# Two cached-attention blocks on one core: where x is transposed for the query projection

## The chip, the core and the metric

One core of a Trainium2 chip runs the whole kernel. The core has a matrix engine (TensorE, PE in the profile, with its weight loads shown apart as PEld), a vector engine (VectorE, DVE), a scalar engine (ScalarE, ACT), a general engine (GpSimd, POOL) and a sync engine (SyncE, SP) that here only issues DMAs. Each engine runs its own list of instructions in order; they wait for one another through semaphores. All data lies in HBM at first; DMAs bring it into SBUF (128 partitions), matmuls write into PSUM (8 banks), and PSUM is read out by VectorE or ScalarE.

The metric is the time of one execution on the device, in microseconds (us): 959.31 us as the median of three runs of the kernel before (958.41 to 959.53).

## The reference

There are two independent blocks, A and B, with the same shapes and their own data; their results are put side by side in the last dimension.

```python
B, Sq, D = 16, 64, 640;  H, Sk, Dh = 32, 512, 128
q = (x @ wq).reshape(B, Sq, H, Dh).transpose(0, 2, 1, 3)
scores = jnp.einsum("bhqd,bhkd->bhqk", q, k_cache) * (Dh ** -0.5)
p = softmax(scores, axis=-1)
o = jnp.einsum("bhqk,bhkd->bhqd", p, v_cache)
out = o.transpose(0, 2, 1, 3).reshape(B, Sq, H * Dh) @ wo      # for A and for B
```

All is bf16. K and V of both blocks are 268 MB of the 295 MB that the core reads, so each element of K and V is loaded once and used once.

## The kernel before

**Tiling.** Two batch rows of 64 queries make one tile of 128 queries. A *step* is one head for such a pair; a *macro step* m is two heads. 16 heads make a *group* of eight macro steps, eight pairs of batch rows make a *pass*, and there are four passes: block A with heads 0 to 15, A with heads 16 to 31, then B in the same way. That gives 32 groups and 256 macro steps. The weights `wq` and `wo` of a pass stay in SBUF for all its groups, in two sets of buffers. The output projection adds up over the 16 heads of a group in PSUM. In the first half of the heads the partial output is kept in SBUF (OVP on ScalarE, L555); in the second half VectorE adds it to the new one (OVF, L560) and ScalarE's queue stores the result.

**A macro step.** The operations, by the names that the code uses: KX transposes K on TensorE (L433), KE evicts it on VectorE (L442). QP2 is the query projection of two heads, ten matmuls (L451), which read x in transposed form from `xT_ring`; QE2 evicts it on ScalarE (L459). SM2 forms the scores (L467); MX takes the negative row maximum on VectorE (L476), EX the exponential with its row sum on ScalarE (L482), RC2 the reciprocal on VectorE (L488), NM the normalization on GpSimd (L496). TR2 transposes the probabilities on TensorE (L505), TE2 evicts them on VectorE (L512), PV2 multiplies with V (L524), OE2 evicts on ScalarE (L532) and OP2 is the output projection (L540 and L545).

**x.** Once in a group, LDX loads the 128 x 640 tile of x as it lies in HBM into `xn_ring`, which has one buffer (NXN = 1). XT transposes it on TensorE in five 128 x 128 pieces into the PSUM bank that TR2 uses too (PTB), and XE copies them on ScalarE into one of the two buffers of `xT_ring` (NX = 2). The group's eight QP2 read them there.

**Order on the engines.** The order on each engine is a written template (PE_T, ACT_T, DVE_T and POOL_T, L30 to L33), run once for every value of a counter k. An entry such as ("QP2", 4) emits the operation for macro step k + 4. On TensorE an iteration is TR2 of k+1, QP2 of k+4, the first half of KX of k+4, SM2 of k+3, PV2 of k+1, XT where one is due, OP2 of k, and the second half of KX of k+4. XT for the group that begins at macro step 8g runs in iteration 8g - 10 (XLEAD = 10), six iterations before its first QP2, between PV2 and OP2.

**Order of the loads.** All loads are issued by SP, in an order that a small planner works out ahead (L189 to L236). Each load has a time at which its buffer should be free, and a due time, both counted in macro steps, and an assumed duration (DMA_NS, L36). The planner's clock begins four steps before the earliest due time. It always takes the load with the earliest due time among those whose buffer is free by its clock (and a small number, the third field, breaks ties), and moves the clock on by the assumed duration. So the due times of x also set where the clock begins. K and V come in chunks of four heads, two DMAs of 512 KB each; five chunks of each fit into the rings (NKB, NVB). The weights come in eight DMAs of 640 KB per pass, as early as the planner finds room.

**Waits.** Dependencies follow from the buffers that each operation reads and writes (L266 to L286). A load waits on SP for the last reader of the buffer that it overwrites: for LDX that is XT of the group before; for K it is KX, for V it is PV2. SP runs in order, so a load that waits holds up all loads behind it.

Of the kernel before, what the change touches and what calls it, by code (L numbers as in the profile page):

```python
# [5 lines left out]
BF16 = mybir.dt.bfloat16  # L6
# [8 lines left out]
class Cfg:  # L15
    G = 4
    HH = 16
    NKB = 5
    NVB = 5
    NX = 2  # L20
    NXN = 1
    XLEAD = 10
    NQ = 2
    NKT = 2
    NP = 4
# [1 line left out]
    NT = 2  # L27
    NO = 2
    NR = 8
    PE_T = (("TR2", 1), ("QP2", 4), ("KX", 4, 0), ("SM2", 3), ("PV2", 1), ("XT", 0), ("OP2", 0), ("KX", 4, 1))  # L30
    ACT_T = (("QE2", 4), ("OE2", 1), ("XE", 0), ("EX", 3, 0), ("EX", 3, 1), ("OV", 0), ("ST", -1))
    DVE_T = (("TE2", 1), ("RC2", 2), ("KE", 4, 0), ("MX", 3, 0), ("MX", 3, 1), ("KE", 4, 1), ("OVF", 0))
    POOL_T = (("NM", 0, 0), ("NM", 0, 1))  # L33
    TAIL_SPLIT = 2
# [4 lines left out]
class Op:  # L39
# [3 lines left out]
    def __init__(self, eng, kind, idx, reads=(), writes=(), dur=0.0, ts=None, aux=None):  # L43
# [13 lines left out]


STAGES = ("LDW", "LDX", "LDK", "LDV", "KX0", "KE0", "KX1", "KE1", "QP2", "QE2", "SM2", "MX0", "MX1", "EX0", "EX1",
          "RC2", "NM0", "NM1", "TR2", "TE2", "XT", "XE", "PV2", "OE2", "OP2", "OV", "ST")  # L60
STAGE_IDX = {s: i for i, s in enumerate(STAGES)}
SUB_KINDS = ("KX", "KE", "EX", "NM", "MX")

# [1 line left out]
def build_plan(dims, cfg):  # L65
# [32 lines left out]
    def make_op(kind, m, sub):  # L98
        g0, g1 = 2 * m, 2 * m + 1
        ps_, bp, grp, h0 = step_info(g0)  # L100
        c = g0 // G
        if kind == "KX":
            return mk("pe", "KX", (m, sub), [("kn", c % cfg.NKB, g0 % G), ("kn", c % cfg.NKB, g1 % G), ("ident",)],
                      [("KTB",)], "KX%d" % sub, m, sub)
        if kind == "KE":
            return mk("dve", "KE", (m, sub), [], [("KTB",), ("ktp", m % cfg.NKT, sub)], "KE%d" % sub, m, sub)
        if kind in ("MX", "EX", "NM"):
            g = 2 * m + sub
            r = g % cfg.NR
            if kind == "MX":  # L110
                return mk("dve", "MX", g, [], [("SB", sub), ("negmax", r)], "MX%d" % sub, m, sub)
            if kind == "EX":
                return mk("act", "EX", g, [("negmax", r)], [("SB", sub), ("p", g % cfg.NP), ("rowsum", r)],
                          "EX%d" % sub, m, sub)
            return mk("pool", "NM", g, [("p", g % cfg.NP), ("recip", r)], [("pn", g % cfg.NPN)], "NM%d" % sub, m, sub)
        r0, r1 = g0 % cfg.NR, g1 % cfg.NR
        if kind in ("XT", "XE"):
            mt = m + cfg.XLEAD
            if mt % MPG != 0 or not (0 <= mt < NMAC):
                return None  # L120
            gq = mt // MPG
            m_ts = mt - cfg.XLEAD + OFF["TR2"]
            if kind == "XT":
                return mk("pe", "XT", gq, [("xn", gq % cfg.NXN), ("ident",)], [("PTB",)], "XT", m_ts, aux=gq)
            return mk("act", "XE", gq, [], [("PTB",), ("xT", gq % cfg.NX)], "XE", m_ts, aux=gq)
        if kind == "QP2":
            return mk("pe", "QP2", m, [("xT", grp % cfg.NX), ("wq", ps_ % 2, h0 // G)], [("QB",)], "QP2", m)
        if kind == "QE2":
            return mk("act", "QE2", m, [], [("QB",), ("qT", m % cfg.NQ)], "QE2", m)
        if kind == "SM2":  # L130
            return mk("pe", "SM2", m, [("qT", m % cfg.NQ), ("ktp", m % cfg.NKT, 0), ("ktp", m % cfg.NKT, 1)],
                      [("SB", 0), ("SB", 1)], "SM2", m)
        if kind == "RC2":
            return mk("dve", "RC2", m, [("rowsum", r0), ("rowsum", r1)], [("recip", r0), ("recip", r1)], "RC2", m)
        if kind == "TR2":
            return mk("pe", "TR2", m, [("pn", g0 % cfg.NPN), ("pn", g1 % cfg.NPN), ("ident",)], [("PTB",)], "TR2", m)
        if kind == "TE2":
            return mk("dve", "TE2", m, [], [("PTB",), ("pT", m % cfg.NT)], "TE2", m)
        if kind == "PV2":
            return mk("pe", "PV2", m, [("pT", m % cfg.NT), ("v", c % cfg.NVB, g0 % G), ("v", c % cfg.NVB, g1 % G)],  # L140
                      [("OB",)], "PV2", m)
        if kind == "OE2":
            return mk("act", "OE2", m, [], [("OB",), ("oT", m % cfg.NO)], "OE2", m)
        if kind == "OP2":
            return mk("pe", "OP2", m, [("oT", m % cfg.NO), ("wo", ps_ % 2, h0 // G)], [("OUTB",)], "OP2", m)
        if kind in ("OV", "OVF", "ST"):
            if h0 + 1 != SPB - 1:
                return None
            last_half = ps_ % NHALF == NHALF - 1
            if kind == "OV":  # L150
                if NHALF == 1:
                    return mk("act", "OV", m, [], [("OUTB",), ("out_sb", grp % 2)], "OV", m, aux=grp)
                if last_half:
                    return None
                return mk("act", "OVP", m, [], [("OUTB",), ("outp", bp)], "OV", m, aux=grp)
            if kind == "OVF":
                if NHALF == 1 or not last_half:
                    return None
                return mk("dve", "OVF", m, [("outp", bp)], [("OUTB",), ("out_sb", grp % 2)], "OV", m, aux=grp)
            if NHALF == 1 or not last_half:  # L160
                return None
            return mk("act", "ST", m, [("out_sb", grp % 2)], [("out_dram", grp)], "ST", m, aux=grp)
        raise ValueError(kind)

    templates = {"pe": cfg.PE_T, "dve": cfg.DVE_T, "pool": cfg.POOL_T, "act": cfg.ACT_T}
    for eng, tmpl in templates.items():
        offs = [t[1] for t in tmpl] + [cfg.XLEAD]
        for k in range(-max(offs), NMAC - min(offs)):
            for t in tmpl:
                kind, off = t[0], t[1]  # L170
                sub = t[2] if len(t) > 2 else 0
                if kind in ("XT", "XE"):
                    op = make_op(kind, k, 0)
                    if op is not None:
                        progs[eng].append(op)
                    continue
                m = k + off
                if 0 <= m < NMAC:
                    op = make_op(kind, m, sub)
                    if op is not None:  # L180
                        progs[eng].append(op)
                        if op.kind == "OV":
                            progs[eng].append(mk("act", "ST", m, [("out_sb", op.aux % 2)], [("out_dram", op.aux)],
                                                 "ST", m, aux=op.aux))
# [20 lines left out]
                                                       aux=(ps_, j), dur=cfg.DMA_NS["LDWO"] * G / 8.0)))  # L205
    for grp in range(NGRP):
        m0 = MPG * grp
        op = mk("sp", "LDX", grp, [], [("xn", grp % cfg.NXN)], "LDX", m0 - cfg.XLEAD + OFF["TR2"], aux=grp,
                dur=cfg.DMA_NS["LDX"])
        ready = NEG if grp < cfg.NXN else MPG * (grp - cfg.NXN) - cfg.XLEAD  # L210
        loads.append((ready, m0 - cfg.XLEAD - 1, 1, op))

    def chunk_pieces(c):
        if c == NCHUNK - 1 and cfg.TAIL_SPLIT > 1:
# [132 lines left out]
def mha_kernel(nc, blocks, out, cfg=None):  # L347
# [15 lines left out]
    prune_waits(progs)  # L363
    NBP, SPB, NHALF = info["NBP"], info["SPB"], info["NHALF"]
    HH = SPB
    NKB, NVB, NX, NXN, NQ, NKT, NP, NPN, NT, NO, NR = (cfg.NKB, cfg.NVB, cfg.NX, cfg.NXN, cfg.NQ, cfg.NKT, cfg.NP,
                                                       cfg.NPN, cfg.NT, cfg.NO, cfg.NR)

    def step_info(g):
# [8 lines left out]
    with contextlib.ExitStack() as es:  # L378
# [6 lines left out]
        wo_sb = sb("wo_sb", [128, 2, HH, DN], BF16)  # L385
        outp = sb("outp", [128, NBP, DN], F32) if NHALF > 1 else None
        xT_ring = sb("xT_ring", [128, NX, KT, 128], BF16)
        xn_ring = sb("xn_ring", [128, NXN, D], BF16)
        kn_ring = sb("kn_ring", [128, NKB, 2, G // 2, 8, DH], BF16)
        v_ring = sb("v_ring", [128, NVB, 2, G, 4, DH], BF16)  # L390
        ktp_ring = sb("ktp_ring", [128, NKT, 2, 2, SK], BF16)
# [202 lines left out]
        def em_LDX(e, op):  # L594
            blk, bp = grp_info(op.aux)
            src = blocks[blk][0][2 * bp:2 * bp + 2].rearrange("b q d -> (b q) d")
            ins = e.dma_start(xn_ring[:, op.aux % NXN, :], src)
            return ins, ins

        def em_XT(e, op):  # L600
            gq = op.aux
            first = last = None
            for kt in range(KT):
                ins = e.transpose(pt_ps_flat[:, kt * 128:(kt + 1) * 128],  # L604
                                  xn_ring[:, gq % NXN, kt * 128:(kt + 1) * 128], ident[:, :])
                first = first or ins
                last = ins
            return first, last

        def em_XE(e, op):  # L610
            gq = op.aux
            ins = e.activation(xT_ring[:, gq % NX].rearrange("p k q -> p (k q)"), pt_ps_flat[:, 0:KT * 128],
                               ACTF.Copy)
            return ins, ins

        def em_LDKV(e, op):
# [6 lines left out]
            else:  # L623
# [4 lines left out]

        emitters = dict(KX=em_KX, KE=em_KE, QP2=em_QP2, QE2=em_QE2, SM2=em_SM2, MX=em_MX, EX=em_EX, RC2=em_RC2,
                        NM=em_NM, TR2=em_TR2, TE2=em_TE2, PV2=em_PV2, OE2=em_OE2, OP2=em_OP2, OV=em_OV,  # L630
                        OVP=em_OVP, OVF=em_OVF, ST=em_ST, XT=em_XT, XE=em_XE, INIT1=em_INIT1, INIT2=em_INIT2,
                        LDWQ=em_LDWQ, LDWO=em_LDWO, LDX=em_LDX, LDK=em_LDKV, LDV=em_LDKV)

        def run_program(e, prog, final_waits=()):
# [85 lines left out]
```

## Time and profile before

| what | value |
|---|---|
| median of 3 runs | 959.31 us (958.41 to 959.53) |
| profiled execution, first to last instruction (span) | 956.8 us |
| TensorE (PE) | 919.4 us busy, 96% |
| VectorE (DVE) | 841.9 us, 88% |
| ScalarE (ACT) | 567.1 us, 59% |
| GpSimd (POOL) | 416.9 us, 44% |
| transposes of x, 160 on TensorE | 14.4 us busy, 222 ns each |
| their evictions, 32 on ScalarE | 22.5 us busy, 702 ns each |
| loads of x, 32 on SP | 160 KB each, 2.5 / 4.3 / 10.5 us from issue to landing (least, median, most) |
| all DMAs | 299.51 MB, 313 GB/s on average |
| granted TensorE clock | 0.998 of full speed |

The profile is of one execution, taken by the hardware. Of that execution the page gives the span; what lies before its first and after its last instruction isn't shown, and the span is 2.5 us below the median of the runs. "Busy" of an engine is the time that its instructions took; "idle before" in a group's line is the time that its engine stood still just before them, with what ended it. In a line such as `ps<-ident,xn_ring` the tile written stands left of the arrow, those read to the right. SPq is the list of DMA issues on SP. A DMA's time "to landing" runs from its issue to the moment when its data is there.

### The profile page before, as it was taken

The numbers are of one execution on the slowest core, as the hardware profiler recorded it, in microseconds if no ns is written. First come the engines' busy times: TensorE is split into PE (matmuls) and PEld (weight loads), VectorE is DVE, ScalarE is ACT, GpSimd is POOL, SyncE is SP. The second block draws the span as 40 slices with busy tenths as digits, with TensorE's granted clock in tenths as the row PEclk, the third lists the DMA queues.
The fourth block names the chain that finished last, engine by engine and source line by source line (L and its number), as shares of the span: only waits on it lengthen the run. The fifth ranks groups of instructions, "written<-read, shape, count | busy, mean of one in ns | idle before, by whom it ended". The sixth has DMA issues, their size and how long they took to land.

```text
span 956.8 us, 34351 instructions
## 1 busy us (share of the span) xinstructions
PE 919.4 (96%) x14755; PEld 733.5 (77%) x15008; DVE 841.9 (88%) x1552; ACT 567.1 (59%) x1585; POOL 416.9 (44%) x518
## 2 busy tenths in 40 slices
PE   4999999999999999999999999999999999999997
PEld 3877777778777777877777787777877778777775
DVE  2898899898899999899999899889899998999996
ACT  1666656666665565656566666666666656565654
POOL 0444444444444444444444444444444444444443
PEclk9999999999999999999999999999999999999999
DMA  9999999999999999888999999988888988899830
GB/s 315 364 365 364 351 365 367 365 368 351 338 337 337 343 330 315 299 292 305 322 332 352 326 353 327 306 294 296 302 305 288 308 301 297 295 297 314 295 124 15
DMA packets 230871, 299.51 MB, mean 313 GB/s; under 512 B 9536, under 2 KB 165184, under 8 KB 230720
## 3 DMA queue, kind: packets, MB, share of 16 engines
q1 hardware_dynamic: 228416, 294.69, 91.0%
q8 instruction: 118, 1.93, 0.8%
q10 hardware_dynamic: 2304, 2.62, 0.8%
q14 instruction: 33, 0.27, 0.1%
HBM read 294.65 MB, written 2.62 MB: 311 GB/s over the span
## 4 chain that ended last, share of the span: by engine, by line
PE 89%; DVE 4%; POOL 3%; issue 2%; SPq 1%; DMA 1%; POOLq 0%; DVEq 0%
PE ps L433 22%; PE ps L524 14%; PE ps L451 14%; PE ps L467 14%; PE ps L505 12%; PE ps L545 7%; PE ps L540 5%; POOL pn_ring L496 3%; DVE out_sb L560 1%; DVE ktp_ring L442 1%; DVE pT_ring L512 1%; PE ps L604 1%; DMA xn_ring<-in_A_x_dram 1%; SPq L626 1%; SPq L583 1%
## 5 line engine op out<-in xcount | busy, mean ns | idle before, releaser
L496 POOL TENSOR_SCALAR pn_ring<-p_ring,recip 128x512 bf16<-128x512 bf16 x512 | 416.3, 843 | 532.7 <-DVE recip L488 532.7
L442 DVE COPY ktp_ring<-ps 128x1024 bf16<-128x1024 bf16 x512 | 353.7, 691 | 105.3 <-PE ps L433 85.1
L482 ACT ACTIVATE p_ring<-ps,negmax 128x512 bf16<-128x512 f32 x512 | 345.6, 684 | 4.8 <-DVE negmax L476 4.8
L476 DVE TENSOR_REDUCE negmax<-ps 128x1 f32<-128x512 f32 x512 | 327.3, 681 | 0.4 <-PE ps L467 0.3
L433 PE MATMUL ps<-ident,kn_ring 128*128 128x128 bf16 x4096 | 314.6, 220 | 2.8 <-DMA kn_ring<-in_A_k_cache_dram 1.6
L532 ACT ACTIVATE oT_ring<-ps 128x256 bf16<-128x256 f32 x256 | 98.0, 383 | 306.0 <-PE ps L524 306.0
L433 PEld LDWEIGHTS ps<-ident,kn_ring 128*128 128x128 bf16 x4096 | 251.9, 98 | 34.2 <-DVE ktp_ring L442 2.6
L524 PEld LDWEIGHTS ps<-pT_ring,v_ring 128*128 128x128 bf16 x4096 | 133.5, 98 | 109.2 <-issue 100.0
L451 PE MATMUL ps<-xT_ring,wq_sb 128*128 128x128 bf16 x2560 | 186.4, 220 | 3.2 <-DMA wq_sb<-in_A_wq_dram 3.2
L512 DVE COPY pT_ring<-ps 128x1024 bf16<-128x1024 bf16 x256 | 174.5, 682 | 4.6 <-PE ps L505 3.8
L524 PE MATMUL ps<-pT_ring,v_ring 128*128 128x64 bf16 x4096 | 163.8, 194 | 3.3 <-issue 1.7
L467 PE MATMUL ps<-ktp_ring,qT_ring 128*64 128x512 bf16 x1024 | 159.8, 392 | 0.4 <-ACT p_ring L482 0.4
L505 PE MATMUL ps<-ident,pn_ring 128*128 128x128 bf16 x2048 | 156.7, 219 | 3.5 <-POOL pn_ring L496 3.5
L451 PEld LDWEIGHTS ps<-xT_ring,wq_sb 128*128 128x128 bf16 x2560 | 155.2, 98 | 3.5 <-DMA wq_sb<-in_A_wq_dram 3.5
L459 ACT ACTIVATE qT_ring<-ps 128x256 bf16<-128x256 f32 x256 | 98.4, 384 | 66.8 <-PE ps L451 66.8
L505 PEld LDWEIGHTS ps<-ident,pn_ring 128*128 128x128 bf16 x2048 | 124.1, 98 | 7.0 <-POOL pn_ring L496 6.7
L545 PE MATMUL ps<-wo_sb,oT_ring 128*128 128x128 bf16 x512 | 112.1, 219 | 13.4
L482 ACT ACTIVATION_READ_ACCUMULATOR p_ring<-ps,negmax 128x1 f32 x512 | 105.0, 205 | 0.0
L540 PE MATMUL ps<-wo_sb,oT_ring 128*128 128x512 bf16 x259 | 97.8, 379 | 0.0
L540 PEld LDWEIGHTS ps<-wo_sb,oT_ring 128*128 128x128 bf16 x512 | 50.1, 98 | 30.6 <-ACT oT_ring L532 0.3
L467 PEld LDWEIGHTS ps<-ktp_ring,qT_ring 128*64 128x64 bf16 x1024 | 36.1, 108 | 27.1 <-ACT p_ring L482 0.6
L545 PEld LDWEIGHTS ps<-wo_sb,oT_ring 128*128 128x128 bf16 x512 | 50.1, 98 | 0.0
(13 smaller groups left out, 112.7 us busy)
## 6 DMA issues: line engine op xcount, KB each, us to landing
kn_ring<-in_A_k_cache_dram SPq DMA_DIRECT2D x128, 512.0 KB, 7.0
v_ring<-in_A_v_cache_dram SPq DMA_DIRECT2D x128, 512.0 KB, 7.2
kn_ring<-in_B_k_cache_dram SPq DMA_DIRECT2D x126, 512.0 KB, 4.8
v_ring<-in_B_v_cache_dram SPq DMA_DIRECT2D x126, 512.0 KB, 5.7
wq_sb<-in_A_wq_dram SPq DMA_DIRECT2D x8, 640.0 KB, 10.4
wo_sb<-in_A_wo_dram SPq DMA_DIRECT2D x8, 640.0 KB, 10.2
wq_sb<-in_B_wq_dram SPq DMA_DIRECT2D x8, 640.0 KB, 8.4
wo_sb<-in_B_wo_dram SPq DMA_DIRECT2D x8, 640.0 KB, 7.5
```

What stands on the lines that cost most here:

```text
L433: ins = e.transpose(kt_ps[:, t8, :], kn_ring[:, c % NKB, j, hp, t8, :], ident[:, :])
L442: ins = e.tensor_copy(dst, src)
L451: ins = e.matmul(q_ps[:, sub * 128:(sub + 1) * 128], wq_sb[:, ps_ % 2, kt, hh * DH:(hh + 1) * DH], xT_ring[:, grp % NX, kt, :], start=(kt ...
L467: ins = e.matmul(s_bank(sub)[64 * j:64 * j + 64, :], qT_ring[:, m % NQ, sub, 64 * j:64 * j + 64], ktp_ring[:, m % NKT, sub, j, :], start=T ...
L476: ins = e.reduce_max(negmax[:, r:r + 1], s_bank(g % 2), axis=AX.X, negate=True)
L482: ins = e.activation(p_ring[:, g % NP, :], s_bank(g % 2), ACTF.Exp, bias=negmax[:, r:r + 1], scale=1.0, accum_out=rowsum[:, r:r + 1])
L496: ins = e.tensor_scalar(dst, src, recip[:, r:r + 1], 1.0, ALU.mult, ALU.mult)
L505: ins = e.transpose(pt_ps[:, sub, t, :], pn_ring[:, g % NPN, t * 128:(t + 1) * 128], ident[:, :])
L512: ins = e.tensor_copy(pT_ring[:, m % NT].rearrange("p s t q -> p (s t q)"), pt_ps_flat)
L524: ins = e.matmul(o_ps[:, col:col + 64], v_ring[:, c % NVB, j, gi, t, :], pT_ring[:, m % NT, sub, t, 64 * j:64 * j + 64], start=(t == 0), s ...
L540: ins = e.matmul(out_ps0, oT_ring[:, m % NO, sub, :], wo_sb[:, ps_ % 2, hh, 0:N0], start=(hh == 0), stop=(hh == SPB - 1))
L545: last = e.matmul(out_ps1, oT_ring[:, m % NO, sub, :], wo_sb[:, ps_ % 2, hh, N0:DN], start=(hh == 0), stop=(hh == SPB - 1))
```

## The change

LDX becomes a transposing DMA: it reads the same 128 x 640 tile of x from HBM and writes it in transposed form into `xT_ring`, where QP2 reads it. `xn_ring`, XT on TensorE and XE on ScalarE go. LDX now waits for the last QP2 that read the `xT_ring` buffer which it overwrites (two groups back), where before it waited for XT. In the planner, x may be loaded ahead for two groups at the start, is due four macro steps before its group's first QP2 is emitted, and goes ahead of everything with the same due time. The first due time of all loads moves from -11 to -8 by this.

```diff
-    NXN = 1
-    XLEAD = 10
+    XLEAD = 4
...
-    PE_T = (("TR2", 1), ("QP2", 4), ("KX", 4, 0), ("SM2", 3), ("PV2", 1), ("XT", 0), ("OP2", 0), ("KX", 4, 1))
-    ACT_T = (("QE2", 4), ("OE2", 1), ("XE", 0), ("EX", 3, 0), ("EX", 3, 1), ("OV", 0), ("ST", -1))
+    PE_T = (("TR2", 1), ("QP2", 4), ("KX", 4, 0), ("SM2", 3), ("PV2", 1), ("OP2", 0), ("KX", 4, 1))
+    ACT_T = (("QE2", 4), ("OE2", 1), ("EX", 3, 0), ("EX", 3, 1), ("OV", 0), ("ST", -1))
...
     for grp in range(NGRP):
         m0 = MPG * grp
-        op = mk("sp", "LDX", grp, [], [("xn", grp % cfg.NXN)], "LDX", m0 - cfg.XLEAD + OFF["TR2"], aux=grp,
-                dur=cfg.DMA_NS["LDX"])
-        ready = NEG if grp < cfg.NXN else MPG * (grp - cfg.NXN) - cfg.XLEAD
-        loads.append((ready, m0 - cfg.XLEAD - 1, 1, op))
+        op = mk("sp", "LDX", grp, [], [("xT", grp % cfg.NX)], "LDX", m0, aux=grp, dur=cfg.DMA_NS["LDX"])
+        ready = NEG if grp < cfg.NX else MPG * (grp - cfg.NX + 1) - 1 - OFF["QP2"]
+        loads.append((ready, m0 - OFF["QP2"] - cfg.XLEAD, -1, op))
...
-        xn_ring = sb("xn_ring", [128, NXN, D], BF16)
...
             src = blocks[blk][0][2 * bp:2 * bp + 2].rearrange("b q d -> (b q) d")
-            ins = e.dma_start(xn_ring[:, op.aux % NXN, :], src)
-            return ins, ins
-
-        def em_XT(e, op):
-            gq = op.aux
-            first = last = None
-            for kt in range(KT):
-                ins = e.transpose(pt_ps_flat[:, kt * 128:(kt + 1) * 128],
-                                  xn_ring[:, gq % NXN, kt * 128:(kt + 1) * 128], ident[:, :])
-                first = first or ins
-                last = ins
-            return first, last
-
-        def em_XE(e, op):
-            gq = op.aux
-            ins = e.activation(xT_ring[:, gq % NX].rearrange("p k q -> p (k q)"), pt_ps_flat[:, 0:KT * 128],
-                               ACTF.Copy)
+            ins = e.dma_start_transpose(xT_ring[:, op.aux % NX, :, :], src)
             return ins, ins
```

More of the change, by code (lines that the diff above doesn't have):

```diff
@@ L59 @@
 STAGES = ("LDW", "LDX", "LDK", "LDV", "KX0", "KE0", "KX1", "KE1", "QP2", "QE2", "SM2", "MX0", "MX1", "EX0", "EX1",
-          "RC2", "NM0", "NM1", "TR2", "TE2", "XT", "XE", "PV2", "OE2", "OP2", "OV", "ST")
+          "RC2", "NM0", "NM1", "TR2", "TE2", "PV2", "OE2", "OP2", "OV", "ST")
 STAGE_IDX = {s: i for i, s in enumerate(STAGES)}
@@ L116, in make_op @@
         r0, r1 = g0 % cfg.NR, g1 % cfg.NR
[L117 to L125, printed above, removed]
         if kind == "QP2":
@@ L166, in build_plan @@
     for eng, tmpl in templates.items():
-        offs = [t[1] for t in tmpl] + [cfg.XLEAD]
+        offs = [t[1] for t in tmpl]
         for k in range(-max(offs), NMAC - min(offs)):
@@ L171, in build_plan @@
                 sub = t[2] if len(t) > 2 else 0
[L172 to L176, printed above, removed]
                 m = k + off
@@ L365, in mha_kernel @@
     HH = SPB
-    NKB, NVB, NX, NXN, NQ, NKT, NP, NPN, NT, NO, NR = (cfg.NKB, cfg.NVB, cfg.NX, cfg.NXN, cfg.NQ, cfg.NKT, cfg.NP,
+    NKB, NVB, NX, NQ, NKT, NP, NPN, NT, NO, NR = (cfg.NKB, cfg.NVB, cfg.NX, cfg.NQ, cfg.NKT, cfg.NP,
                                                        cfg.NPN, cfg.NT, cfg.NO, cfg.NR)
@@ L630, in mha_kernel @@
                         NM=em_NM, TR2=em_TR2, TE2=em_TE2, PV2=em_PV2, OE2=em_OE2, OP2=em_OP2, OV=em_OV,
-                        OVP=em_OVP, OVF=em_OVF, ST=em_ST, XT=em_XT, XE=em_XE, INIT1=em_INIT1, INIT2=em_INIT2,
+                        OVP=em_OVP, OVF=em_OVF, ST=em_ST, INIT1=em_INIT1, INIT2=em_INIT2,
                         LDWQ=em_LDWQ, LDWO=em_LDWO, LDX=em_LDX, LDK=em_LDKV, LDV=em_LDKV)
```

## The prediction

> **What bounds the kernel now.** First the page: engine shares and the chain of work that ended last.
>
> ```profile
> span 956.8 us, 34351 instructions
> PE 919.4 (96%) x14755; PEld 733.5 (77%) x15008; DVE 841.9 (88%) x1552; ACT 567.1 (59%) x1585; POOL 416.9 (44%) x518
> PE 89%; DVE 4%; POOL 3%; issue 2%; SPq 1%; DMA 1%; POOLq 0%; DVEq 0%
> ```
>
> TensorE is busy 96% of the span and carries 89% of the chain. What it runs in order sets the time, and work taken out of its list can be worth its length there. Next, the groups of instructions that go:
>
> ```profile
> L612 ACT ACTIVATE xT_ring<-ps 128x640 bf16<-128x640 bf16 x32 | 22.5, 702 | 7.4 <-PE ps L604 7.4
> L604 PE MATMUL ps<-ident,xn_ring 128*128 128x128 bf16 x160 | 14.4, 222 | 7.6 <-DMA xn_ring<-in_A_x_dram 7.6
> ```
>
> ScalarE's 22.5 us lie on an engine that idles 41% of the span, so I give them nothing. What the 32 transposes cost TensorE is read from the timeline, in the starts of the query projection (L451), which runs once in each macro step:
>
> ```profile
> 395.04 0.72 PE L451 MATMUL ps<-xT_ring,wq_sb 128*128 128x128 bf16 x10
> ...
> 398.61 0.72 PE L451 MATMUL ps<-xT_ring,wq_sb 128*128 128x128 bf16 x10
> ...
> 400.74 0.44 PE L604 MATMUL ps<-ident,xn_ring 128*128 128x128 bf16 x5
> ...
> 402.45 0.72 PE L451 MATMUL ps<-xT_ring,wq_sb 128*128 128x128 bf16 x10
> ...
> 406.02 0.72 PE L451 MATMUL ps<-xT_ring,wq_sb 128*128 128x128 bf16 x10
> ```
>
> Steps of 3.57, 3.84 and 3.57 us: the one with the transposes is 0.27 to 0.28 longer, less than their 0.44, since the output projection behind them would have waited for the OE2 eviction anyway. Last, the start and the loads:
>
> ```profile
> 18.42 0.62 PE L467 MATMUL ps<-ktp_ring,qT_ring 128*64 128x512 bf16 x4
> 23.28 0.45 PE L604 MATMUL ps<-ident,xn_ring 128*128 128x128 bf16 x5 [4.23 <-DMA xn_ring<-in_A_x_dram]
> ```
> ```profile
> L626 SPq DMA_DIRECT2D kn_ring<-in_A_k_cache_dram x1: 1060/1060/1060, 48.0 to 48.0; - x1
> ...
> DMA to landing us min/median/max: 9.0/9.0/9.0
> ```
> ```profile
> 58.76 0.61 PE L433 MATMUL ps<-ident,kn_ring 128*128 128x128 bf16 x8
> ```
> ```profile
> 120.00:237.00 117.00, 115.26 (x1876) 92.30 (x1906) 105.58 (x196) 71.87 (x202) 53.18 (x66) 1.00 1.07 363
> 700.00:940.00 240.00, 234.63 (x3784) 186.79 (x3848) 217.98 (x403) 143.03 (x403) 107.26 (x132) 1.00 0.82 274
> ```
>
> TensorE stands 4.23 us for the second group's x; K chunk 6 lands at 48.0+9.0 = 57.0 and is first transposed at 58.76, a lead of only 1.7. So the loads nearly bind for the first 60 us. Until 237 us they run at 363 GB/s, which I take for the queue's ceiling; later 274 suffice.
>
> **Removed: XT and XE.** Of the 32 XT, the first runs before the first projection and the second is the stall at 23.28. The other 30 lie in steps like the one shown: 30 x 0.28 = 8.4 us. Nothing refills the place: steps without XT in the same groups already run at 3.57. XE is worth nothing by itself; its cover is ScalarE's wait for PV2 (306.0 us idle at L532), and without that cover it would be 22.5.
>
> **Removed: the stall at the start.** Without XT for group 1, the KX transposes behind it follow at about 19.04, and TR2 of step 0 at about 20.0, when its normalized rows are ready (POOL: 18.40+1.62), against 24.53: 4.5 us earlier. That isn't kept, because K and V then arrive late. Leads read in the same way (last issue plus its landing, against first use): K chunk 3 2.9 us, chunk 4 2.6, V chunk 3 2.5, K chunk 5 2.2, V chunk 4 2.0, K chunk 6 1.7, K chunk 7 3.1. TensorE can move up only by the smallest, with one correction: group 2's x now goes behind V chunk 4 and K chunk 6 on SP. At the ceiling an x of 163,840 B takes 163,840/363 GB/s = 0.45, so those two land 0.45 earlier: leads of 2.4 and 2.15. I take 2.1. What is late next is K chunk 6.
>
> **Added: 32 transposing loads on SP.** No row of before shows one. From below: the direct load's 0.45 us of queue, so extra e = 0; a fully free load, e = -0.45, is the end below nothing. From above, for a queue that merely empties around it: the first x load, alone on the queue, lives 2.45 us from issue to landing (0.79 to 3.25), so e = 2.45-0.45 = 2.0. From far above: its five 128x128 parts each live 2.45, one after another: 12.2 us, e = 11.8. I take e = 1.0, the middle of the two near rows: the bytes and queue are those of the direct load, but something has to turn the elements. The far end keeps its place as a rival.
>
> At the start, x of groups 0 and 1 go ahead of K chunk 6 (net 2.1-2e) and that of group 2 ahead of K chunk 7 (net 3.1-3e): with e = 1.0 both leave +0.1. Later an extra microsecond is hidden. A group's eight steps take 28.5 us; its K and V are 8.39 MB (23.1 us at 363 GB/s), weights 0.66 MB (1.8 us, in the first three passes), x 0.45, output 0.45 (second half of heads only): 25.4 to 25.8, room 3.1 before output; without weights 24.0, room 5. Without that room e would count in full, 32 us.
>
> **Moved: order and waits on SP.** LDX no longer waits for XT (38.8 us of SP's idle time, 23 times, at most 2.0) but for the last QP2 that reads the xT buffer, step 8g-9. Queued behind it stands K chunk 4g, whose buffer comes free in the same iteration through KX, at its end; so LDX holds up nothing that could go. x then has nine steps, 32 us, until its QP2, against at most 10.5 us of landing now: hidden, exposed only beyond 32. By the planner's arithmetic its clock starts at -12 rather than -15 steps, so pass 1's weights move from behind K chunk 8 to around K chunk 22; their use is step 64, at about 235 us. That spreads them and relieves K and V after 60 us: nothing, where no load is late. On POOL only INIT stays ahead of NM, as before; ACT's stores keep their place.
>
> **Sum.** 8.4 + 0.1 = 8.5 us: the profiled execution goes from 956.8 to 948.3. The median 959.31 stands 2.5 over that span, and I carry that over: 950.8. With e from -0.45 to 2.0: gains of 8.4+3.0 = 11.4 (947.9) to 8.4+3.1-6.0 = 5.5 (953.8).
>
> **The skill against the rows.** The row: five TensorE transposes take 0.44 us here and cost 0.28. The Trainium skill, "VectorE: DVE Perf Modes", section "The three transpose paths", gives the DMA crossbar 1309 ns for 128x128 bf16 against TensorE's 390, and its rules prefer TensorE where PSUM will do: five parts in a row would be 6.5 us, my estimate from that page, and the third rival's sum with e = 6.1 some 1038 us. Its page "DMA: Bandwidth & Descriptors", section "Latency and other measured facts", gives 261 GB/s for transposing transfers, an estimated 0.63 us, e = 0.2: 949.2. No run here shows either.
>
> **Rivals.**
> - *The extra eats most of the gain (e of 2.0 to 3.1).* Start: 3.1-3e = -2.9 to -6.2, so gains of 5.5 to 2.2: 953.8 to 957.1. For it: the leads of 1.7 to 3.1. Against: the queue would have to empty at every x, though SP issues ahead of it.
> - *The gain doesn't appear (958 to 960).* VectorE has about 3.5 us of work in a 3.57 step and could bind instead. Against: neighbouring steps already hold 3.57 with it.
> - *Slower: the transposing load holds the one queue that K and V use.* It decides at e = 3.1, where the room in a group of the first three passes is used up; just above, some 3.2, the sum turns. Three of their 24 groups are the start. With the five parts two at a time, 6.1 us, e = 5.7: 14 at the start, 21 x 2.6 = 55, last pass 8 x 0.7 = 6, less 8.4: +66, 1026 us. One at a time, e = 11.8: 32 + 21 x 8.7 + 8 x 6.8 - 8.4 = +261, 1220. For it: x shares SP's queue with every K and V load, at 363 GB/s in the first quarter. Against: it is one instruction of 160 KB.
>
> **How the numbers follow.** Forecast 0.62; small extra e to 3.1, 0.08; no gain 0.03; slower 0.27. About 0.2%, 1.9 us, is what a measurement tells from no change. Faster: 0.62 + 0.08 = 0.70; same 0.03; slower 0.27. The forecast's own range is 947.9 to 953.8. To leave out no more than 2 in 10, I go from 947.5 up into the slower case to 985 (e about 4.3: 9.8 + 21 x 1.2 = 35, less 8.4, +27); above that lies about 0.18.
>
> **What would show it.** L604 and L612 gone; every step of 3.84 at 3.57; TR2 of step 0 near 20 us, then TensorE waiting briefly for K chunks 3 to 6; x's issue to landing below 32 us; K and V near 363 GB/s in the first quarter. Wrong, if TensorE waits for kn_ring or v_ring loads after 60 us, if SP is held at LDX, or if queue shares rise while GB/s fall.

## The result, and the profile after

The changed kernel takes 949.88 us (median of four runs, 949.83 to 950.03) against 958.86 us (957.75 to 959.53) for the kernel before, measured beside it: a ratio of 0.9909, 95% interval 0.9895 to 0.9923, some 9 us faster. The forecast was 950.8. On another chip it took 949.71 us against 958.82 (0.9903, 0.9887 to 0.9920).

The page of the changed kernel: the span, the engines and the shares of the chain.

```profile
span 948.0 us, 34249 instructions
PE 923.9 (97%) x14848; PEld 724.0 (76%) x14848; DVE 841.6 (89%) x1552; ACT 549.2 (58%) x1553; POOL 416.5 (44%) x518
PE 89%; DVE 4%; POOL 3%; SPq 3%; DMA 1%; issue 1%; POOLq 0%; DVEq 0%
```

TensorE bounds the kernel as before; SP's share of the chain has grown from 1% to 3%. (The busy time of PE isn't lower because the trace of before lacks half of the matmul records of L540: 259 of 512. In their place its page shows 13.4 us of idle time before L545, and 919.4 + 13.4 = 932.8 would be 8.9 more than now.) The span fell by 8.8 us. The timeline of TensorE around 390 us, the starts of the query projection (L434 in this kernel), in the group that was shown of before:

```profile
387.72 0.72 PE L434 MATMUL ps<-xT_ring,wq_sb 128*128 128x128 bf16 x10
...
391.28 0.72 PE L434 MATMUL ps<-xT_ring,wq_sb 128*128 128x128 bf16 x10
...
394.85 0.72 PE L434 MATMUL ps<-xT_ring,wq_sb 128*128 128x128 bf16 x10
...
398.42 0.72 PE L434 MATMUL ps<-xT_ring,wq_sb 128*128 128x128 bf16 x10
```

Every step is 3.56 to 3.57 us; the one of 3.84 is gone. The first projection of group 2 and the last projection of all, before and now:

```profile
72.47 0.72 PE L451 MATMUL ps<-xT_ring,wq_sb 128*128 128x128 bf16 x10
940.71 0.72 PE L451 MATMUL ps<-xT_ring,wq_sb 128*128 128x128 bf16 x10
```
```profile
71.81 0.72 PE L434 MATMUL ps<-xT_ring,wq_sb 128*128 128x128 bf16 x10
931.92 0.72 PE L434 MATMUL ps<-xT_ring,wq_sb 128*128 128x128 bf16 x10
```

Between them lie 868.24 and 860.11 us: 8.1 us less, 29 steps of 0.28. It is the same in every group behind the start: eight macro steps took 28.81 us and now take 28.53, and 29.33 and 29.05 in the second half of the heads. The other 0.66 us lie before group 2. Counted as the prediction counts, 0.28 of them are one more removed XT and 0.4 us are what the start itself gave; the split is bookkeeping, since TensorE waits for loads there. Why the start gave so little is seen in TensorE's timeline:

```profile
20.81 0.62 PE L488 MATMUL ps<-ident,pn_ring 128*128 128x128 bf16 x8 [0.18 <-POOL pn_ring L479]
```
```profile
32.25 0.72 PE L434 MATMUL ps<-xT_ring,wq_sb 128*128 128x128 bf16 x10
35.05 1.01 PE L416 MATMUL ps<-ident,kn_ring 128*128 128x128 bf16 x8 [2.07 <-DMA kn_ring<-in_A_k_cache_dram]
35.99 1.06 PE L450 MATMUL ps<-ktp_ring,qT_ring 128*64 128x512 bf16 x4
36.99 1.03 PE L507 MATMUL ps<-pT_ring,v_ring 128*128 128x64 bf16 x16
```

TR2 of step 0 runs at 20.81 instead of 24.53: the stall for x is gone. At 33 us TensorE has caught up with the loads and waits 2.07 us for K chunk 3. The three groups of matmuls after that wait take 1.01 to 1.06 us instead of 0.61 to 0.64. K chunk 7 then lands at 65.10 us, 0.1 us ahead of its use. That is as close as K chunk 3, which TensorE waited for, and its transposition begins 0.16 us later in its step than in others: a short wait as well. The loads themselves, from the view of the tile `xT_ring`:

```profile
L580 SPq DMA_TRANSPOSE xT_ring<-in_A_x_dram x16: 1325/3911/5066, 0.8 to 414.2; - x16
L580 SPq DMA_TRANSPOSE xT_ring<-in_B_x_dram x16: 1199/1206/2807, 443.0 to 874.6; - x16
...
DMA to landing us min/median/max: 3.1/8.6/10.6
```

The numbers are the durations of the issue on SP in ns (least, median, most). By the medians a transposing load held SP for 3.9 us in block A and for 1.2 in block B, where less is queued; in `e5_copies1`, an experiment told of below that keeps the queue fuller in B too, it is 3.9 there as well. The plain load took 0.62 and 0.34. Landing takes at most 10.6 us, far from the 32 that x has. The queue's row, and five-microsecond windows around the second x load (engines busy with counts, then granted clock, DMA share and GB/s):

```profile
q1 hardware_dynamic: 245312, 294.69, 98.7%
```
```profile
10.00:15.00 5.00, 3.34 (x31) 3.11 (x32) 1.38 (x2) 0.20 (x1) 0.00 (x0) 1.00 1.07 371
15.00:20.00 5.00, 4.53 (x40) 2.77 (x38) 3.48 (x7) 1.91 (x6) 0.87 (x2) 1.00 1.16 263
20.00:25.00 5.00, 4.63 (x77) 3.78 (x78) 4.94 (x10) 3.23 (x9) 2.38 (x3) 1.00 1.06 372
```

The window with the transposing load moves 263 GB/s, its neighbours 371 and 372: 108/372 of 5 us, 1.45 us of queue lost. The x of group 2, between 55 and 60 us, gives 265 GB/s. From 120 to 237 us the rate is 345 GB/s where it was 363, and TensorE doesn't wait.

### The profile page after: what moved, and what is told of

Same layout as the page of the kernel before. It is cut to its first block, busy times and chain, and to the rows that moved or that the text cites. A ratio compares the mean times of both kernels' runs of the same rounds, so it can differ in the third digit from the quotient of the medians.

```text
span 948.0 us, 34249 instructions
## 1 busy us (share of the span) xinstructions
PE 923.9 (97%) x14848; PEld 724.0 (76%) x14848; DVE 841.6 (89%) x1552; ACT 549.2 (58%) x1553; POOL 416.5 (44%) x518
## 3 DMA queue, kind: packets, MB, share of 16 engines
q1 hardware_dynamic: 245312, 294.69, 98.7%
## 4 chain that ended last, share of the span: by engine, by line
PE 89%; DVE 4%; POOL 3%; SPq 3%; DMA 1%; issue 1%; POOLq 0%; DVEq 0%
PE ps L416 22%; PE ps L507 14%; PE ps L434 14%; PE ps L450 14%; PE ps L488 11%; PE ps L523 11%; POOL pn_ring L479 3%; PE ps L528 3%; DVE out_sb L543 1%; DVE ktp_ring L425 1%; DVE pT_ring L495 1%; DMA kn_ring<-in_A_k_cache_dram 1%; SPq L593 1%; SPq L580 1%; SPq L589 1%
## 5 line engine op out<-in xcount | busy, mean ns | idle before, releaser
L434 PE MATMUL ps<-xT_ring,wq_sb 128*128 128x128 bf16 x2560 | 186.1, 220 | 7.7 <-DMA wq_sb<-in_A_wq_dram 7.7
L523 PE MATMUL ps<-wo_sb,oT_ring 128*128 128x512 bf16 x512 | 167.1, 380 | 0.3 <-DMA wo_sb<-in_A_wo_dram 0.3
L434 PEld LDWEIGHTS ps<-xT_ring,wq_sb 128*128 128x128 bf16 x2560 | 154.9, 98 | 7.7 <-DMA wq_sb<-in_A_wq_dram 7.7
```

Source lines behind the costliest of these rows:

```text
L434: ins = e.matmul(q_ps[:, sub * 128:(sub + 1) * 128], wq_sb[:, ps_ % 2, kt, hh * DH:(hh + 1) * DH], xT_ring[:, grp % NX, kt, :], start=(kt ...
L523: ins = e.matmul(out_ps0, oT_ring[:, m % NO, sub, :], wo_sb[:, ps_ % 2, hh, 0:N0], start=(hh == 0), stop=(hh == SPB - 1))
```

## The experiments

Diffs are against the changed kernel, unless said otherwise.

**Is the gain TensorE's place in the step?** `e2_xt_kept` puts the work of TensorE and ScalarE back, on data that is always there; `e6_xt_only` leaves the eviction out again.

```diff
+            if kind == "XT":
+                return mk("pe", "XT", gq, [("ident",)], [("PTB",)], "XT", m_ts, aux=gq)
+            return mk("act", "XE", gq, [], [("PTB",), ("xd", 0)], "XE", m_ts, aux=gq)
...
+                ins = e.transpose(pt_ps_flat[:, kt * 128:(kt + 1) * 128], ident[:, :], ident[:, :])
...
+            ins = e.activation(xd[:, :], pt_ps_flat[:, 0:KT * 128], ACTF.Copy)
```

> The changed kernel with the five TensorE transposes and the ScalarE eviction of each group put back at their old places, on data that is always there (the identity), written to a buffer that nobody reads: TensorE and ScalarE carry their old load, nothing waits for x in the old way, the DMAs are those of the changed kernel. Theory (the gain is TensorE's place in the step): every group has one step of 3.84 again, 31 x 0.28 = 8.7 us, so 958.6 us. Rival (the gain came from the loads' order, or from the stall at the start): about 950 us. In between, if ScalarE or the shared PSUM bank gave part of it in another way.

> The changed kernel with the five TensorE transposes of each group put back as in e2_xt_kept, on the identity, but without the ScalarE eviction: nobody reads what they write. Theory (the 0.28 us are TensorE's place in its order): the step is 3.84 to 3.85 again and the time that of e2_xt_kept, 958.1 us. Rival (it was the hand-over of the PSUM bank to ScalarE and back that lengthened the step): 3.57 and about 950 us.

Measured: 958.10 us (957.71 to 958.29) and 958.29 (957.77 to 958.39), both the same as the kernel before (ratios 0.9994, 0.9985 to 1.0003, and 0.9995, 0.9987 to 1.0004). The steps of `e2_xt_kept` and, below, of `e6_xt_only`, in TensorE's timeline:

```profile
398.14 0.72 PE L450 MATMUL ps<-xT_ring,wq_sb 128*128 128x128 bf16 x10
...
400.27 0.44 PE L602 MATMUL ps<-ident 128*128 128x128 bf16 x5
...
401.99 0.72 PE L450 MATMUL ps<-xT_ring,wq_sb 128*128 128x128 bf16 x10
```
```profile
398.21 0.72 PE L450 MATMUL ps<-xT_ring,wq_sb 128*128 128x128 bf16 x10
...
400.34 0.44 PE L602 MATMUL ps<-ident 128*128 128x128 bf16 x5
...
402.06 0.72 PE L450 MATMUL ps<-xT_ring,wq_sb 128*128 128x128 bf16 x10
```

3.85 us each, with the eviction and without. The five transposes alone cost the 0.28; ScalarE's 0.70 and the hand-over of the PSUM bank cost nothing. Of the 8.7 us expected 8.2 came back. From the first projection of group 2 to the last `e2_xt_kept` needs 868.24 us, exactly as the kernel before; the two transposes put back in the start cost 0.2 us together (group 2 begins at 72.01 against 71.81), since TensorE waits for loads there anyway.

**What do the transposing loads cost at the start?** `e1_plain` loads x as it lies (its transposition is left out), `e8_first3_plain` does so for the first three groups alone.

```diff
-            ins = e.dma_start_transpose(xT_ring[:, op.aux % NX, :, :], src)
+            ins = e.dma_start(xT_ring[:, op.aux % NX].rearrange("p k q -> p (k q)"), src)
```
```diff
+            if op.aux < 3:
+                ins = e.dma_start(xT_ring[:, op.aux % NX].rearrange("p k q -> p (k q)"), src)
+                return ins, ins
             ins = e.dma_start_transpose(xT_ring[:, op.aux % NX, :, :], src)
```

> The changed kernel with a plain load in place of the transposing one: x lands as it lies in HBM, so the query projection multiplies data that was not transposed; everything else is as in the changed kernel. This is the change with an extra e = 0. Theory (the transposing load costs the queue more than a plain one, and only the first 60 us have no room for it): the start keeps 2.1 us of gain where the changed kernel keeps 0.4 (its first projection of the third group stands at 71.81 against 72.47, of which 0.28 is a removed transpose), so 949.9 - 1.7 = 948.2 us; K and V loads go back from 345 to about 363 GB/s between 120 and 237 us; steps stay at 3.57. Rival (the transposing load costs the queue no more than a plain one, and the start is held by something else): 949.9 us, and the rate stays near 345 GB/s.

> The changed kernel with plain loads for x of groups 0 to 2 alone (that x is left untransposed, the other 29 groups are computed as in the reference). Theory (only the three loads of the start cost anything, the other 29 are hidden in the queue's room): the time of e1_plain, 947.3 us. Rival (the 29 later ones cost something too): between 947.3 and 949.9 us; 949.9 if the start is not what differs.

Measured: `e1_plain` 947.32 us (946.73 to 947.93; ratio 0.9879, 0.9866 to 0.9893), `e8_first3_plain` 947.83 (946.42 to 948.63; 0.9881, 0.9866 to 0.9896), beside the changed kernel's 949.71 on the same chip as the latter. The same windows in `e1_plain`, and its rate between 120 and 237 us:

```profile
10.00:15.00 5.00, 4.00 (x36) 3.57 (x38) 1.38 (x2) 0.38 (x1) 0.00 (x0) 1.00 1.07 367
15.00:20.00 5.00, 3.89 (x42) 2.15 (x42) 4.13 (x8) 1.79 (x6) 1.52 (x2) 1.00 1.09 361
20.00:25.00 5.00, 4.67 (x80) 3.96 (x80) 4.92 (x10) 3.73 (x11) 1.71 (x3) 1.00 1.07 365
```
```profile
120.00:237.00 117.00, 115.27 (x1877) 92.46 (x1906) 106.47 (x197) 70.97 (x201) 53.17 (x66) 1.00 1.05 358
```

With plain loads the dip to 263 isn't there, and the group-2 projection starts at 68.64 us, 3.2 before the changed kernel's. By the medians the three transposing loads of the start cost 1.9 us (`e8_first3_plain` beside the changed kernel on one chip) to 2.6 (`e1_plain`, on another chip). The intervals of `e8_first3_plain` and of the changed kernel, both taken against the kernel before, meet at their ends; the four times of each do not (at most 948.63, at least 949.43). That the other 29 loads cost the time nothing is seen directly: from the first projection of group 2 to the last, the changed kernel needs 860.11 us, `e1_plain` 860.09 and `e8_first3_plain` 860.12. The profiled executions spread more than the medians: `e1_plain` and `e8_first3_plain` issue the same loads up to 73 us, and yet group 2 begins at 68.64 in the one and at 70.49 in the other. The last section says what this difference consists of.

**Does it matter where x stands among the first loads?**

```diff
-    XLEAD = 4
+    XLEAD = 1
```

> The changed kernel with x due one macro step before its first projection is emitted, not four: at the start x of group 1 goes behind K chunk 3 and x of group 2 behind K chunk 7. Theory (the start is bound by the arrival of K and V, and each transposing load ahead of a chunk delays it): K chunk 3 lands about 1 us earlier and K chunk 7 about 1 us earlier; the smallest lead is then K chunk 6 with 0.7 us, so 0.7 to 0.9 us faster than the changed kernel, 949.0 us. Rival (the order of x doesn't matter at the start, the sum of bytes does): 949.9 us. Slower than 950.5 only if x itself comes late.

Measured: 949.64 us (949.20 to 950.29), no difference that can be told. K chunk 3 did land at 33.5 us instead of 34.9, and group 1 began at 40.77 instead of 43.11; but x of group 1 then stood ahead of the chunks behind it, K chunk 6 landed at 58.1 instead of 57.3, and group 2 began at 71.91 against 71.81. The time is the rival's. But the order did do something: K chunk 7, with one x less ahead of it, landed at 63.65 us instead of 65.10. What was won there was lost at K chunk 6, which had the same loads ahead of it and came 0.8 us later; about half of that is a longer lag between its bytes and its landing (1.8 against 1.4 us, see the last section). Why it lagged isn't shown, so the rival's reason isn't either.

**Do the later weights take part in it?**

```diff
-    t_now = min(e[1] for e in loads) - 4.0
+    t_now = min(e[1] for e in loads) - 7.0
```

> The changed kernel with the planner's clock begun three steps earlier, as it began before the change: the weights of the second pass are loaded from behind K chunk 8 on again, not from about K chunk 22. Theory (moving the weights is worth nothing, since no load is late there): 949.9 us, at most 0.5 more, because the leads of K chunks 8 to 10 are 1.6 to 4.3 us and a 640 KB weight load takes 1.8 of them. Rival (the later weights are a hidden part of the gain): 951 to 953 us, with waits of TensorE for K or V after 60 us.

Measured: 949.90 us (949.82 to 949.94). The leads behind the start fall, that of K chunk 15 from 8.1 to 2.4 us, and K chunk 8, now behind a load of weights, comes late:

```profile
72.37 0.61 PE L416 MATMUL ps<-ident,kn_ring 128*128 128x128 bf16 x8 [0.20 <-DMA kn_ring<-in_A_k_cache_dram]
```

That step takes 3.93 us instead of 3.57, and from the first projection of group 2 to the last TensorE needs 860.48 us rather than 860.11. The time doesn't show these 0.4 us because group 2 began that much earlier in this execution (71.45 against 71.81; 71.38 in the changed kernel's second profile, so the start's own spread is as large). The later weights are thus worth at most 0.4 us, not the 1 to 3 of the rival.

**Where does the hidden cost come out?** `e5_copies1` and `e5_copies3` issue each transposing load of groups 4 to 29 once or three times more, into a spare buffer; `e5_plain3` does the latter with plain loads. In all three the partial sums of the first half of the heads are kept in bf16.

```diff
+        if cfg.XC_FROM <= grp < NGRP - 2:
+            for i in range(cfg.NXC):
+                op = mk("sp", "LDXC", (grp, i), [], [("xc", i)], "LDX", m0, sub=1 + i, aux=(grp, i),
+                        dur=cfg.DMA_NS["LDX"])
+                loads.append((ready, m0 - OFF["QP2"] - cfg.XLEAD, -0.9 + 0.01 * i, op))
...
+            ins = e.dma_start_transpose(xc_ring[:, op.aux[1], :, :], src)
```

> The changed kernel with every transposing load from group 4 to 29 issued a second time, into a spare buffer that nobody reads (the partial sums kept between the halves of the heads are bf16 for room). Theory (a transposing load takes about 2.0 us of the queue, from the packets of the changed kernel's trace, and is hidden while the queue has room): a group with weights then needs 23.1 + 1.8 + 0.45 + 2 x 2.0 = 29.4 us of queue against 28.5 to 29.0 of work, and the lead of 7 us at group 4 covers most of it: 950 to 955 us. Rival (it costs no more than a plain load, 0.45): 949.9 us with leads as in the changed kernel.

> As e5_copies1 with three extra transposing loads a group. Theory (2.0 us of queue each, the queue becomes the bound): 23.1 + 1.8 + 0.45 + 4 x 2.0 = 33.4 against 28.5 to 29.0 in groups 4 to 23, 31.6 against 29.0 in 24 to 29: some 95 + 15 us, less the lead, so about 1050 us. Rival (0.45 each): room for all, 950 us. Far more than 1050, if SP's own time for the issue (3.9 us each while the queue is full) adds up: 26 x 3 x 3.9 = 304, so up to 1250.

> As e5_copies3, but the three extra loads of x a group are plain ones. Theory (it is the transposition that takes the queue's time, 1.6 us a load there, and a plain one takes 0.45): a group needs 1.35 us more, which the room covers: 949.9 us. Rival (the number of loads or SP's issues cost the time): near the 996.4 us of e5_copies3.

Measured: 949.53 us (949.40 to 949.65), 996.44 (995.34 to 997.54; ratio 1.0395, 1.0376 to 1.0414) and 950.89 (950.71 to 951.07). The waits of TensorE for loads in `e5_copies3`, and a window (its rate last):

```profile
PE ps L426 <- DMA kn_ring<-in_A_k_cache_dram: 15.6, 6, 7.2
PE ps L426 <- DMA kn_ring<-in_B_k_cache_dram: 13.3, 5, 5.0
...
PE ps L533 <- DMA wo_sb<-in_B_wo_dram: 5.9, 1, 5.9
```
```profile
237.00:360.00 123.00, 111.27 (x1742) 86.41 (x1742) 99.08 (x182) 63.70 (x181) 48.67 (x60) 0.96 1.09 316
```

With one extra load, two transposing loads a group, all is hidden. With four a group TensorE waits up to 7.2 us at a time, and the kernel is slower than before. The expected 1050 was too much: next to one another transposing loads took 1.58 us of queue each (the time of their packets over 16 engines), not 2.0. With that a group needs 23.1 + 1.8 + 0.45 + 4 x 1.58 = 31.7 us, 3 more than it has, over 20 groups 60, less a lead of 7 to 12 us: near the measured 46.6. This is a balance of the whole, not the place of the loss: TensorE loses the time in two groups at each change of pass (38.3 and 34.2 us for groups 8 and 9, 37.3 and 37.0 for 16 and 17, 35.4 and 36.0 for 24 and 25), where the weights are loaded, and from group 2 on all others take 28.53 or 29.05 us as in the changed kernel. The planner counts the extra loads and therefore also issues a pass's weights later and closer together: those of the second pass at 218 to 280 us in `e5_copies3` and at 208 to 264 in `e5_plain3`, against 143 to 257. `e5_plain3` has this as well and costs 1.0 us rather than 46.6, so it is the transposition that costs, and not the count of loads or their order. Its 1.0 us is still more than the theory's nothing. TensorE waited once, 1.2 us, for a K chunk of block B (at 748 us, behind a change of pass), where leads had shrunk to about 1 us. Whether the moved weights or the queue did that wasn't tried.

**A version between the two.** `e7_mixed` transposes x of groups 0 to 2 on TensorE, where it waits for loads anyway, and loads the other 29 transposed.

```diff
+    XTLEAD = 6
+    XPE = 3
...
+        if grp < cfg.XPE:
+            op = mk("sp", "LDX", grp, [], [("xn", 0)], "LDX", m0 - cfg.XTLEAD + OFF["TR2"], aux=grp,
+                    dur=cfg.DMA_NS["LDX"])
+            loads.append((NEG, m0 - OFF["QP2"] - cfg.XLEAD, -1, op))
+            continue
```

> The changed kernel with the first three groups' x loaded plainly and transposed on TensorE (into xT_ring, evicted by ScalarE, six iterations' lead in place of ten, so that XT of group 1 comes after its x), the other 29 by the transposing load. Theory (the transposing load costs 1 us and more of the queue, which only the first 60 us have no room for, and TensorE waits there anyway): the start of e1_plain, 2.6 us better than the changed kernel, 947.3 us, with steps of 3.57 from about 70 us on. Rival (the start is held by something else than the three transposing loads): 949.9 us. Slower than that, if XT at its new place stops TensorE again.

> The changed kernel as it is, once more, beside the next two on the same chip: 949.9 us if it repeats.

> e7_mixed once more, beside the changed kernel on the same chip: 948.4 us, 1.5 faster than the changed kernel, if the difference is one of the kernels and not of the chips; 949.9 if it isn't.

Measured: 948.35 us (947.30 to 948.82; ratio to before 0.9892, 0.9879 to 0.9906), then 949.00 (948.15 to 949.64; 0.9894, 0.9879 to 0.9909) beside 949.71 (949.43 to 950.05; 0.9903, 0.9887 to 0.9920) of the changed kernel. It beats the kernel before. Against the changed kernel it is 0.7 to 1.5 us ahead by the medians, and group 2 begins earlier in its two profiled executions (70.51 and 70.62 us, against 71.81 and 71.38); but the intervals overlap, so that it is faster is not shown.

## Why the prediction was right

- *Removed XT: 30 x 0.28 = 8.4 us.* Right in place and size: 29 steps gave 8.1, the thirtieth lies in the start. `e2_xt_kept` and `e6_xt_only` show that it is TensorE's place, and ScalarE's 22.5 us nothing. The rival that the gain doesn't appear, with VectorE as the bound, fell: every group is 0.28 us shorter. But the reason given for 0.28 instead of 0.44, that the output projection would have waited for an eviction, is wrong. In the changed kernel it follows PV2 without a gap (the lines below). The busy time of a group of matmuls includes the run-out of its last ones, during which the next group has begun: the ten matmuls of the projection show 0.72 us and the next group starts 0.56 after them, the eight transposes of K 0.61 and 0.45. Each of them thus takes 0.056 us of TensorE's place, and five transposes of x 0.28.

```profile
392.94 0.64 PE L507 MATMUL ps<-pT_ring,v_ring 128*128 128x64 bf16 x16
393.41 0.38 PE L523 MATMUL ps<-wo_sb,oT_ring 128*128 128x512 bf16 x1
```

- *Removed stall: not kept, because K and V bind.* Right. TR2 of step 0 came at 20.81 rather than 20.0, and TensorE then waited for K chunk 3. What was late next was named wrongly: not K chunk 6 (lead 0.7 now) but K chunk 3 and V chunk 1, then K chunk 7, with leads of 0.1. With plain loads it is K chunk 6, as said (`e1_plain`: lead 0.1, K chunk 7 1.1).
- *Start: +0.1 us with e = 1.0.* Measured 0.4, in part by luck. With e = 1.45 as measured, the prediction's own formula gives 3.1 - 3 x 1.45 = -1.25 us. What offset it was not foreseen: K chunk 7 landed 1.95 us behind the bytes moved, where in the kernel before it was 3.3 (last section), and that is 1.3 us of room. The difference between plain and transposing loads there was put at 2.1 - 0.1 = 2.0 us; `e1_plain` and `e8_first3_plain` give 2.6 and 1.9.
- *Added load, e = 1.0 us of queue.* Too small, and within its ends of -0.45 to 2.0: the window's dip says 1.45, the packets 2.07 - 0.45 = 1.6. The start also had more room than the 2.1 us taken (`e1_plain` kept 3.55 in its profiled execution). Neither figure of the Trainium skill that was weighed fits this load, whose 2.07 us are 79 GB/s. The page "DMA: Bandwidth & Descriptors", section "Latency and other measured facts", gives 261 GB/s for a non-contiguous middle dimension (350 to 400 for the contiguous case): an estimated 0.63 us for x, too short. The page "VectorE: DVE Perf Modes", section "The three transpose paths", gives 1309 ns for 128x128: an estimated 6.5 us for five in a row, too long.
- *Later hidden.* Right: 860.1 us from group 2 on, with transposing loads and with plain ones (`e1_plain`, `e8_first3_plain`). But the sign given for it, K and V near 363 GB/s in the first quarter, failed: 345, with q1's share up from 91.0% to 98.7%. That falling rates would show the prediction wrong was itself wrong, since a rate may fall as long as no lead runs out. SP's longer issue, up to 5.1 us, wasn't foreseen and hides in the same leads.
- *Moved weights and SP's waits: nothing.* Nearly right: with the weights in their old order one K chunk comes late and costs 0.4 us (`e4_clock`).
- *The slower rival, from e = 3.1.* The mechanism is real: `e5_copies3` shows it, with e = 4 x 1.58 - 0.45 = 5.9. The extra loads lie in groups 4 to 29, for which the formula gives 20 x 2.8 + 6 x 0.9 = 61 us; measured are 46.6 over the changed kernel. The formula left out the lead of 7 to 12 us that must be used up first, and so the point lies above 3.1: `e5_copies1`, with some 2 x 1.83 - 0.45 = 3.2, is still free. (The room of 5 without weights leaves the output out; the 24.0 beside it counts it, which leaves 4.5.)

## What to carry to other kernels

Read what an instruction on the bounding engine costs from the length of its step with and without it, not from its busy time: 0.28 us here, not 0.44, and next to nothing where that engine waits for loads. A load that takes more of a queue is free as long as leads last, so price it by the stretch in which leads are near zero, here the start; and compute the point from which the room is gone before calling it hidden.

## What the runs showed of the hardware that was not expected

**In most transposing loads sixteen packets stop together.** The packets of x are then 256 bytes, 640 a load, with a median of 18 ns. In the load of the changed kernel that passes at 280.6 us, sixteen of these packets begin within 0.05 us of one another and take 1.45 to 1.47 us each. Over all 32 loads the short ones make 0.72 us of each engine's time per load and the long ones 1.35; the 1.45 us that the windows lose agree with that. The stop isn't part of every such load: in the first, alone on the queue, no packet takes over 0.3 us (0.9 us of each engine's time in all), and in those at 819 and 848 us none over 0.7. So its length depends on what else is in the queue, and 2.07 us is no fixed price. That the load waits until all 16 engines have come up to it would fit; it is argued, and wasn't tried.

**Landing can lag behind the bytes.** Put against the time at which the queue had moved as many bytes as were issued up to a load, loads at the start of `e1_plain` land 1.5 us later; in the kernel before the lag grows from 2.2 to 3.9 us at V chunk 1 (29.7 us) and stays above 3 to the end of the 70 us looked at, at the same rate. The trace records a landing in 16 steps, without naming engines. Of the 32 steps of the two loads of V chunk 1, 31 had come by 27.47 us and the last came at 29.73: one straggler held the chunk back by 2.3 us. Which one it is, and why, isn't shown. In one pair this is all of the start's spread: of `e1_plain` and `e8_first3_plain`, with the same loads there, K chunk 6, the last that binds in both, lands 1.49 us behind its bytes in the first and 3.34 in the second, and group 2 begins by the same 1.85 us later. After each of the two transposing loads at 19 and 58 us the lag is down to 0.6 to 0.7 us, and back near 2 some 8 us later; the 16 steps of each load of V chunk 5, just behind the second of them, lie within 0.13 us.

**After a wait TensorE may go on slower, or not.** After the wait of 2.07 us at 33 us the next groups of matmuls took 1.0 us instead of 0.62, and the granted clock of that five-microsecond window (35 to 40) is 0.66. The step was 3.7 us longer than the others, not 2.1. The same followed waits of 2.06 to 2.09 us there in three more profiles (the changed kernel's second, `e4_clock` and `e5_plain3`). But `e5_copies1`, which issues the same loads up to that place, goes on at full speed, with a granted clock of 1.00:

```profile
34.55 0.61 PE L426 MATMUL ps<-ident,kn_ring 128*128 128x128 bf16 x8 [2.08 <-DMA kn_ring<-in_A_k_cache_dram]
35.09 0.62 PE L460 MATMUL ps<-ktp_ring,qT_ring 128*64 128x512 bf16 x4
```

So the length of the wait alone doesn't decide it. It didn't change the time here either: group 2 begins at 71.33 us in `e5_copies1` and at 71.38 and 71.81 in the changed kernel, since K chunk 7 is waited for behind it.
